# P transposes and softmax sums moved behind the eighth K tile of a decode-attention batch

## The chip, the cores and the metric

The kernel runs on one core of a Trainium2 chip. The metric is device time in microseconds (us) of that core, the median over several executions. One execution is recorded by the hardware profiler; its trace gives every instruction's start and duration on TensorE (PE, with weight loads apart as PEld), VectorE (DVE), ScalarE (ACT), GpSimd (POOL), and the DMA issues of SyncE (SP).

## The reference

One decode step (one new token) for a batch of 8: pre-norm attention over the last 2048 positions of a KV cache, then an MLP with a shift over tokens, both with residuals. With one token the shifted branch of the MLP is all zeros, so w1 and w2 drop out.

```
x = A_x                                   # [8, 1, 512]
q = layernorm(x) @ wq                     # 32 heads of 128
k, v = last W = 2048 rows of the caches   # 8 kv heads, 4 q heads share one
p = softmax(q k^T / sqrt(128));  o = p v
h = x + o @ wo
xb = layernorm(h)
x1 = xb + 0                               # shift of a length-1 sequence
out = h + x1 + gelu(layernorm(x1) @ w3) @ w4
```

All inputs are bfloat16. K and V of one batch are 4.2 MB each (8 heads x 2048 x 128 x 2 bytes), 67 MB for all batches; with wq, wo, w3 and w4 the traffic is 79.18 MB.

## The kernel before

**Loads.** SyncE issues all large loads on one queue, in a fixed order (`sp_prog`, line 234 on): wq, the two K halves of batch 0 (each half is 4 kv heads, 2 MB, one of two slots), then per batch the two K halves of the next batch and the two V halves of this one, at last the rest of wo, w3 and w4. There are two K slots and two V slots. The next load of a K slot waits until TensorE has transposed the tiles in it (`sem_Thi`, waited for ahead of line 246: 4 tiles for the first slot, 8 for the second); a load of a V slot waits until TensorE has used it (`sem_PV`). w4 goes into the first K slot and so waits for the fourth tile of the last batch (line 265).

**A batch on TensorE** (`pe_block`, line 561). A K half is cut into 4 tiles of 16 blocks of 128 positions. `pe_T` (line 438) transposes a tile's 16 blocks into one of two PSUM buffers `kT_ps`; ScalarE copies the lower half to SBUF (`act_Elo`, line 460), VectorE the upper (`dve_Ehi`, line 464). `pe_QK` (line 478) multiplies the transposed tile with the queries, 4 heads side by side, and adds into the scores `S_ps`. After the eighth tile VectorE takes the maximum (`dve_max`, line 487 on), ScalarE the exponential in two halves with row sums (`act_exp`, line 503).

The probabilities of a batch are used one batch later: `pe_P` (line 454) transposes P, 8 blocks a half, into `kT_ps`; `dve_pT` (line 525) multiplies with a mask into `pT_sb`; `pe_LB` (line 510) adds the row sums over partitions and `dve_rL` (line 516) inverts them; `pe_PV` (line 535) multiplies with V; `dve_O1` and `pe_OP` (lines 544, 554) scale and reorder the output, and `act_OP` stores it.

**The order around the change.** The program of each engine is written out by hand as a list. TensorE's batch is a loop body; its waits (`need`, line 421) consume semaphores by constants, so that the body is the same in each pass. Before the change TensorE's order in a batch is: tiles 0 to 3; P halves 0 and 1; sums; scores of tiles 0 and 1; then tiles 4 to 7, each followed by the scores of the tile two before; scores 6 and 7; PV and output of the last batch. VectorE copies tiles 0 to 3, does both mask multiplies and the reciprocal, and copies tiles 4 to 7. As `pe_P` writes into `kT_ps`, tiles 4 and 5 wait for the mask multiplies (`sem_pT`).

After the loop come the last batch's P, PV and output (`pe_last`), the projection with wo (line 668), the norms, w3 (line 733), gelu, and w4 (line 761).

Of the kernel before, what the change touches and what calls it, by code (L numbers as in the profile page):

```python
# [28 lines left out]
NT = 4  # L29
# [7 lines left out]
def bass_sequential_preLN__sliding_block_cached__mixer_s_mlp__decode_kernel(  # L37
# [24 lines left out]
    with es:  # L62
# [99 lines left out]
        sem_pT = S("sem_pT")  # L162
# [110 lines left out]
        PE, AC, DV = [], [], []  # L273
# [135 lines left out]
        def dve_qc(e, b):  # L409
            e.tensor_copy(qcur[:, :, 32 - R:32], q_all[:, b, :].rearrange("p (g r) -> p g r", r=R)).then_inc(sem_qc, 1)  # L410
# [4 lines left out]
        def need(e, sem, n):  # L415
            d = n - taken.setdefault(sem, 0)
            if d > 0:
                taken[sem] = n
                log.append((sem, d))
                if e is not None:  # L420
                    e.wait_ge(sem, d).then_inc(sem, -d)  # L421

        def pe_T(e, i, t):
            p = 2 * NT * i + t
            gq = t // NT
            if t % NT == 0:
                need(e, sem_k[gq], 16 * (i + 1))
            if t in (4, 5):
                need(e, sem_pT, 2 * i + t - 3)
            elif t in (2, 3, 6, 7):  # L430
                need(e, sem_Elo, p - 1)
                need(e, sem_Ehi, p - 1)
            if e is None:
                return
            k0 = t % NT * CT * DH
            src = slots[:, gq, k0:k0 + CT * DH]
            for c in range(CT):
                ins = e.matmul(kT_ps[t % 2][:, c * 128:(c + 1) * 128], src[:, c * 128:(c + 1) * 128],  # L438
                               perm_b[:, :], is_transpose=True)
                if c == CT // 2 - 1:  # L440
                    ins.then_inc(sem_Tlo, 1)
                if c == CT - 1:
                    ins.then_inc(sem_Thi, 1)

        def pe_P(e, i, half):
            need(e, sem_exp, 2 * i + half + 1)
            n = min(2 * NT * i + 3 + half, 2 * NT * NB)
            need(e, sem_Elo, n)
            need(e, sem_Ehi, n)
            if e is None:  # L450
                return
            for c in range(CT // 2):
                k = half * CT // 2 + c
                ins = e.matmul(kT_ps[half][:, c * 128:(c + 1) * 128], P_sb[:, k * 128:(k + 1) * 128],  # L454
                               perm_p[:, :], is_transpose=True)
            ins.then_inc(sem_PT, 1)

        def act_Elo(e, i):
            e.wait_ge(sem_Tlo, i + 1)
            e.activation(kT_sb[:, i % NKT, 0:W // 2], kT_ps[i % 2][:, 0:W // 2], ACT.Copy).then_inc(sem_Elo, 1)  # L460

        def dve_Ehi(e, i):
            e.wait_ge(sem_Thi, i + 1)
            e.tensor_copy(kT_sb[:, i % NKT, W // 2:W], kT_ps[i % 2][:, W // 2:W]).then_inc(sem_Ehi, 1)  # L464

        def pe_QK(e, i):
            b, t = divmod(i, 2 * NT)
            gq, qi = divmod(t, NT)
            need(e, sem_Elo, i + 1)
            need(e, sem_Ehi, i + 1)  # L470
            if t == 0:
                need(e, sem_qc, b + 1)
            if e is None:
                return
            kv = kT_sb[:, i % NKT, :].rearrange("d (c g p) -> d g c p", p=PP, g=GL)
            o = 32 - R - R * t
            for gl in range(GL):
                ins = e.matmul(S_ps[32 * gl:32 * (gl + 1), 0, :], qcur[:, GL * gq + gl, o:o + 32],  # L478
                               kv[:, gl, :, :], start=(t == 0), stop=(t == 2 * NT - 1),
                               tile_position=(0, 32 * gl), skip_group_check=True)  # L480
            ins.then_inc(sem_QK, 1)
# [18 lines left out]
        def act_exp(e, b, half):  # L500
            e.wait_ge(sem_max, b + 1)
            n = 512 // 2
            e.activation(P_sb[:, half * W // 2:(half + 1) * W // 2].rearrange("r (k g) -> r k g", g=GL),  # L503
                         bass.AP(tensor=S_ps[:, :, :].tensor, offset=half * n, ap=[[1024, 128], [1, n], [0, GL]]), ACT.Exp,
                         bias=mtile[:, 0, 0:1], scale=1.0, accum_out=lsum[:, half:half + 1]).then_inc(sem_exp, 1)

        def pe_LB(e):
            if e is not None:
                for half in range(2):
                    ins = e.matmul(LB, lspread[:, :, :].rearrange("p q h -> p (q h)"), lsum[:, half:half + 1],  # L510
                                   start=(half == 0), stop=(half == 1))
                ins.then_inc(sem_LB, 1)

        def dve_rL(e, b):
            e.wait_ge(sem_LB, b + 2)
            e.reciprocal(rL[:, :], LB).then_inc(dve_self, 1)
            cnt["dve_self"] += 1

        def dve_pT(e, b, half):
            e.wait_ge(sem_PT, 2 * b + half + 3)  # L520
            if b < 0 and half == 0:
                e.wait_ge(sem_pool, POOL_PT)
            m = mask16[:, :, :]
            h0 = half * CT // 2
            e.tensor_tensor(bass.AP(tensor=pT_sb[:, :, :, :].tensor, offset=h0 * NT * 48,  # L525
                                    ap=[[CT * NT * 48, 128], [48, CT // 2 * NT], [32, 2], [1, 16]]),
                            kT_ps[half][:, 0:W // 2].rearrange("p (c a x) -> p c a x", a=2, x=16),
                            bass.AP(tensor=m.tensor, offset=m.offset, ap=[m.ap[0], [0, CT // 2 * NT], [0, 2], [1, 16]]),
                            ALU.mult).then_inc(sem_pT, 1)

        def pe_PV(e, slot, gq, cs=range(CT)):
            for c in cs:
                for q in range(NT):
                    k = q * CT + c
                    ins = e.matmul(pv_ps[32 * q:32 * (q + 1), :], pT_sb[:, c, q, 16 * gq:16 * gq + 32],  # L535
                                   slots[:, slot, k * DH:(k + 1) * DH], start=(gq == 0 and c == 0),
                                   stop=(gq == 1 and c == CT - 1), tile_position=(0, 32 * q), skip_group_check=True)
            if c == CT - 1:
                ins.then_inc(sem_PV[gq], 1)
# [9 lines left out]
        def pe_OP(e, b):  # L549
            need(e, sem_O1, b + 1)  # L550
            if e is None:
                return
            for q in range(4):
                ins = e.matmul(op_ps(b), selw[:, q, :], o_sum[:, NJ * q:NJ * (q + 1)], start=(q == 0), stop=(q == 3))  # L554
            ins.then_inc(sem_OP, 1)
# [4 lines left out]

        def pe_block(e, i, later=None):
            p = 2 * NT * i
            for t in range(NT):
                pe_T(e, i, t)
            pe_P(e, i, 0)
            pe_P(e, i, 1)
            pe_LB(e)
            pe_QK(e, p)
            pe_QK(e, p + 1)
            for t in range(NT, 2 * NT):  # L570
                pe_T(e, i, t)
                pe_QK(e, p + t - 2)
            pe_QK(e, p + 6)
            pe_QK(e, p + 7)
            if i == 0:
                return
            with nullcontext() if e is None else e.If_ne(later, 0):
                log.append("later")
                for gq in range(2):
                    need(e, sem_v[gq], 16 * i)  # L580
                    if e is not None:
                        pe_PV(e, 2 + gq, gq)
                pe_OP(e, i - 1)
# [18 lines left out]
        for i in range(NB):  # L602
            p = 2 * NT * i
            for t in range(2 * NT):
                AC.append(lambda e, n=p + t: act_Elo(e, n))
                DV.append(lambda e, n=p + t: dve_Ehi(e, n))
                if t == 3:
                    DV.append(lambda e, i=i: dve_pT(e, i - 1, 0))
                    DV.append(lambda e, i=i: dve_pT(e, i - 1, 1))
                    if i:  # L610
                        DV.append(lambda e, i=i: dve_rL(e, i - 1))
            AC.append(lambda e, i=i: act_exp(e, i, 0))
            AC.append(lambda e, i=i: act_exp(e, i, 1))
            DV.append(lambda e, i=i: dve_max(e, i))
            if i + 1 < NB:
                DV.append(lambda e, i=i: dve_qc(e, i + 1))
            if i:
                DV.append(lambda e, i=i: dve_O1(e, i - 1))
                AC.append(lambda e, i=i: act_OP(e, i - 1))
# [211 lines left out]
```

## Time and profile before

| | |
|---|---|
| median of 4 runs | 193.66 us (193.16 to 194.82) |
| the profiled execution's own time | 193.32 us |
| its span, first to last instruction | 191.5 us |
| TensorE busy | 141.9 us (74%) |
| VectorE, ScalarE busy | 85.8 us (45%), 93.3 us (49%) |
| GpSimd busy | 6.4 us (3%) |
| mean granted TensorE clock | 0.916 |

A row of the page's groups names the line, the engine, the operation, what it writes and reads, how often, and the busy time; behind the bar stand the idle time of the engine just before and what ended it. In a timeline the columns are start, duration, engine, line, operation and the number of instructions merged into the row, with the wait before it in brackets. SPq is SyncE's queue of DMA issues, PEq TensorE's sequencer. A slice is a fortieth of the span, its digit the busy share in tenths.

| group | instructions | busy us | mean ns |
|---|---|---|---|
| K tile transposes, line 438 | 1024 | 72.7 | 233 |
| scores, line 478 | 256 | 22.6 | 387 |
| PV, line 535 | 1024 | 16.2 | 219 |
| P transposes, line 454 | 144 | 10.9 | 218 |
| sums, line 510 | 36 | 5.0 | 243 |
| lower copies on ScalarE, line 460 | 64 | 64.8 | 1024 |
| upper copies on VectorE, line 464 | 64 | 44.2 | 691 |
| mask multiplies on VectorE, line 525 | 18 | 12.4 | 687 |

Matmuls overlap in the array, so that the mean of one is longer than the distance between two.

### The profile page before, as it was taken

What the parts mean: (1) busy time and instruction counts of PE and PEld (TensorE: products, weight loads), DVE (VectorE), ACT (ScalarE), POOL (GpSimd) and SP (SyncE); (2) the same over time, 40 slices, a digit from 0 to 9 for tenths busy, and PEclk for the clock granted to TensorE, in tenths of its full rate; (3) what the DMA queues carried; (4) which work ended last, traced back from release to release, by engine and by line L of the source; (5) the groups of instructions that cost most, each with busy time, mean ns of one, the idle gap of its engine ahead of it and who ended that gap; (6) DMA issues with size and microseconds to landing.
All of it is one profiled execution on the core that took longest, in us unless ns stands there. A gap on an engine that the chain in (4) does not pass through costs nothing. (4 is left out here: it accounts for less than half of the span.)

```text
span 191.5 us, 6348 instructions
## 1 busy us (share of the span) xinstructions
PE 141.9 (74%) x2848; PEld 114.8 (60%) x2848; DVE 85.8 (45%) x183; ACT 93.3 (49%) x119; POOL 6.4 (3%) x17
## 2 busy tenths in 40 slices
PE   2037893499859995997499949994997499987664
PEld 0014771487658765774497749674875397676652
DVE  7924745064615461744055514551746045551041
ACT  3032664465466446664284457455854464552041
POOL 8400000000000000000000000000000000000000
PEclk9999999589997999999879996999999979999755
DMA  6999999999999999999999999999999999999991
GB/s 221 438 428 431 424 417 431 435 431 435 431 436 424 421 431 433 431 438 431 435 431 424 424 435 431 438 431 438 428 428 424 431 431 438 435 435 407 409 401 42
DMA packets 6329, 79.31 MB, mean 414 GB/s; under 512 B 672, under 2 KB 688, under 8 KB 1712
## 3 DMA queue, kind: packets, MB, share of 16 engines
q1 hardware_dynamic: 6304, 79.18, 97.2%
q8 instruction: 6, 0.10, 0.2%
q10 hardware_dynamic: 16, 0.01, 0.0%
q14 instruction: 3, 0.02, 0.0%
HBM read 79.18 MB, written 0.01 MB: 413 GB/s over the span
## 5 line engine op out<-in xcount | busy, mean ns | idle before, releaser
L460 ACT ACTIVATE kT_sb<-kT_ps 128x1024 bf16<-128x1024 bf16 x64 | 64.8, 1024 | 50.0 <-PE kT_ps L438 49.7
L438 PE MATMUL kT_ps<-perm_b,slots 128*128 128x128 bf16 x1024 | 72.7, 233 | 17.2 <-PEq L421 17.0
L438 PEld LDWEIGHTS kT_ps<-perm_b,slots 128*128 128x128 bf16 x1024 | 65.2, 105 | 27.7 <-issue 27.4
L464 DVE COPY kT_sb<-kT_ps 128x1024 bf16<-128x1024 bf16 x64 | 44.2, 691 | 68.2 <-PE kT_ps L438 68.2
L503 ACT ACTIVATE P_sb<-S_ps,mtile 128x1024 bf16<-128x1024 f32 x16 | 17.7, 1110 | 19.3 <-DVE mtile L498 19.3
L478 PE MATMUL S_ps<-kT_sb,qcur 128*32 128x512 bf16 x256 | 22.6, 387 | 2.9 <-PEq L421 2.9
L535 PE MATMUL misc<-slots,pT_sb 128*32 128x128 bf16 x1024 | 16.2, 219 | 1.8 <-PEq L421 1.8
L535 PEld LDWEIGHTS misc<-slots,pT_sb 128*32 128x32 bf16 x1024 | 14.7, 97 | 3.3 <-issue 3.2
L525 DVE TENSOR_TENSOR pT_sb<-kT_ps,mask 128x1024 bf16<-128x1024 bf16 x18 | 12.4, 687 | 3.6 <-PE kT_ps L454 3.5
L454 PE MATMUL kT_ps<-perm_p,P_sb 128*128 128x128 bf16 x144 | 10.9, 218 | 3.1 <-PEq L421 3.1
L478 PEld LDWEIGHTS S_ps<-kT_sb,qcur 128*32 128x32 bf16 x256 | 5.5, 93 | 10.1 <-issue 6.6
L454 PEld LDWEIGHTS kT_ps<-perm_p,P_sb 128*128 128x128 bf16 x144 | 8.4, 97 | 5.1 <-issue 4.6
L554 PE MATMUL b<-o_sum,selw 128*128 128x32 f32 x56 | 7.3, 275 | 4.3 <-PEq L421 4.3
L554 PEld LDWEIGHTS b<-o_sum,selw 128*128 128x128 f32 x56 | 6.8, 191 | 5.3 <-issue 5.3
L487 DVE TENSOR_REDUCE mtile<-S_ps 128x1 f32<-128x512 f32 x8 | 5.5, 692 | 5.0 <-PE S_ps L478 5.0
L286 DVE TENSOR_SCALAR ident_f<-iota_f 128x128 f32<-128x128 f32 x1 | 5.7, 5684 | 1.3 <-POOL iota_f L207 1.3
L287 DVE TENSOR_SCALAR ident_b<-iota_f 128x128 bf16<-128x128 f32 x1 | 5.6, 5609 | 0.0
L344 PE MATMUL b<-ident_b,xln_b 8*128 8x8 bf16 x4 | 0.3, 175 | 7.1 <-DVE xln_b L320 7.1
L544 DVE TENSOR_SCALAR o_sum<-misc,rL 128x128 f32<-128x128 f32 x8 | 2.8, 351 | 5.6 <-PE misc L535 5.6
L668 PE MATMUL S_ps<-opl,slots 128*128 128x8 bf16 x128 | 3.6, 167 | 2.0 <-issue 1.8
L510 PE MATMUL S_ps<-lsum,lspread 128*128 128x1 f32 x36 | 5.0, 243 | 0.0
L344 PEld LDWEIGHTS b<-ident_b,xln_b 8*128 8x128 bf16 x4 | 0.2, 115 | 8.0 <-DVE xln_b L320 8.0
(91 smaller groups left out, 64.9 us busy)
## 6 DMA issues: line engine op xcount, KB each, us to landing
slots<-in_A_k_cache_dram SPq DMA_DIRECT2D x16, 2048.0 KB, 13.9
slots<-in_A_v_cache_dram SPq DMA_DIRECT2D x16, 2048.0 KB, 17.9
slots<-in_A_wq_dram SPq DMA_DIRECT2D x1, 4096.0 KB, 12.2
slots<-in_A_wo_dram SPq DMA_DIRECT2D x2, 1024.0 KB, 21.9
slots<-in_A_wo_dram SPq DMA_DIRECT2D x1, 2048.0 KB, 26.7
slots<-in_B_w_dram SPq DMA_DIRECT2D x2, 896.0 KB, 31.5
slots<-in_B_w_dram SPq DMA_DIRECT2D x1, 1024.0 KB, 28.6
slots<-in_B_w_dram SPq DMA_DIRECT2D x1, 512.0 KB, 28.3
```

Of the source, the lines that this page charges most:

```text
L286: e.tensor_single_scalar(ident_f[:], iota_f[:], 0.0, ALU.is_equal)
L287: ins = e.tensor_single_scalar(ident_b[:], iota_f[:], 0.0, ALU.is_equal)
L438: ins = e.matmul(kT_ps[t % 2][:, c * 128:(c + 1) * 128], src[:, c * 128:(c + 1) * 128], perm_b[:, :], is_transpose=True)
L454: ins = e.matmul(kT_ps[half][:, c * 128:(c + 1) * 128], P_sb[:, k * 128:(k + 1) * 128], perm_p[:, :], is_transpose=True)
L460: e.activation(kT_sb[:, i % NKT, 0:W // 2], kT_ps[i % 2][:, 0:W // 2], ACT.Copy).then_inc(sem_Elo, 1)
L464: e.tensor_copy(kT_sb[:, i % NKT, W // 2:W], kT_ps[i % 2][:, W // 2:W]).then_inc(sem_Ehi, 1)
L478: ins = e.matmul(S_ps[32 * gl:32 * (gl + 1), 0, :], qcur[:, GL * gq + gl, o:o + 32], kv[:, gl, :, :], start=(t == 0), stop=(t == 2 * NT - ...
L487: ins = e.tensor_reduce(mtile[:, 1, 0:1], S_ps[:, 0, :], AX.X, ALU.max)
L503: e.activation(P_sb[:, half * W // 2:(half + 1) * W // 2].rearrange("r (k g) -> r k g", g=GL), bass.AP(tensor=S_ps[:, :, :].tensor, offset ...
L525: e.tensor_tensor(bass.AP(tensor=pT_sb[:, :, :, :].tensor, offset=h0 * NT * 48, ap=[[CT * NT * 48, 128], [48, CT // 2 * NT], [32, 2], [1, ...
L535: ins = e.matmul(pv_ps[32 * q:32 * (q + 1), :], pT_sb[:, c, q, 16 * gq:16 * gq + 32], slots[:, slot, k * DH:(k + 1) * DH], start=(gq == 0 ...
L554: ins = e.matmul(op_ps(b), selw[:, q, :], o_sum[:, NJ * q:NJ * (q + 1)], start=(q == 0), stop=(q == 3))
```

## The change

In TensorE's batch the two P halves and the sums leave their place between the fourth and fifth tile. The tiles run from 0 to 7 without a break, from the third on each is followed by the scores of the tile two before; then P half 0, the sums, the scores of tile 6, P half 1, the scores of tile 7. Tiles 4 and 5 no longer wait for the mask multiplies but, as the others, for the copies of the tile two before; P waits for the copies of tiles 6 and 7 in place of 2 and 3. Ahead of PV stands a wait for both mask multiplies. On VectorE the multiplies and the reciprocal stand behind the copy of tile 7, ahead of the maximum.

```
         def pe_T(e, i, t):
...
-            if t in (4, 5):
-                need(e, sem_pT, 2 * i + t - 3)
-            elif t in (2, 3, 6, 7):
+            if t > 1:
                 need(e, sem_Elo, p - 1)
                 need(e, sem_Ehi, p - 1)
...
         def pe_P(e, i, half):
             need(e, sem_exp, 2 * i + half + 1)
-            n = min(2 * NT * i + 3 + half, 2 * NT * NB)
+            n = min(2 * NT * i + 7 + half, 2 * NT * NB)
...
         def pe_block(e, i, later=None):
             p = 2 * NT * i
-            for t in range(NT):
-                pe_T(e, i, t)
-            pe_P(e, i, 0)
-            pe_P(e, i, 1)
-            pe_LB(e)
-            pe_QK(e, p)
-            pe_QK(e, p + 1)
-            for t in range(NT, 2 * NT):
+            pe_T(e, i, 0)
+            pe_T(e, i, 1)
+            for t in range(2, 2 * NT):
                 pe_T(e, i, t)
                 pe_QK(e, p + t - 2)
+            pe_P(e, i, 0)
+            pe_LB(e)
             pe_QK(e, p + 6)
+            pe_P(e, i, 1)
             pe_QK(e, p + 7)
+            need(e, sem_pT, 2 * i + 2)
...
             for t in range(2 * NT):
                 AC.append(lambda e, n=p + t: act_Elo(e, n))
                 DV.append(lambda e, n=p + t: dve_Ehi(e, n))
-                if t == 3:
-                    DV.append(lambda e, i=i: dve_pT(e, i - 1, 0))
-                    DV.append(lambda e, i=i: dve_pT(e, i - 1, 1))
-                    if i:
-                        DV.append(lambda e, i=i: dve_rL(e, i - 1))
+            DV.append(lambda e, i=i: dve_pT(e, i - 1, 0))
+            DV.append(lambda e, i=i: dve_pT(e, i - 1, 1))
+            if i:
+                DV.append(lambda e, i=i: dve_rL(e, i - 1))
```

## The prediction

> **What bounds the kernel now.** I read the page's slices and queues first, then the chain that ended last, then the DMA issues with their landing times, and last the timeline of one batch and of the tail. The slices and the queue of the page:
>
> ```profile
> DMA  6999999999999999999999999999999999999991
> GB/s 221 438 428 431 424 417 431 435 431 435 431 436 424 421 431 433 431 438 431 435 431 424 424 435 431 438 431 438 428 428 424 431 431 438 435 435 407 409 401 42
> q1 hardware_dynamic: 6304, 79.18, 97.2%
> ```
>
> The reader is to see that the 16 DMA engines are full in every slice but the first and the last, at 417 to 438 GB/s until the weights (407, 409, 401). One queue carries the 79.18 MB; at the 430 GB/s that the table of stretches has from 20 to 180 us (last column; the one before it is the engines' busy share) they take 184.1 us of a span of 191.5.
>
> ```profile
> 20.00:180.00 160.00, 128.26 (x2595) 106.05 (x2596) 71.04 (x144) 85.29 (x105) 0.00 (x0) 0.94 1.01 430
> ```
>
> TensorE is busy 74%, and it waits for K at the head of every batch. The end of the chain of waits:
>
> ```profile
> 152.98 5.21 PE kT_ps L438 x64
> 158.19 0.02 issue
> 158.21 1.49 SPq L265
> 159.69 0.04 issue
> 159.73 28.32 DMA slots<-in_B_w_dram
> ```
>
> The chain says that the first four K tiles of the last batch release the w4 loads (line 265), which land 28 us later and end the run. Those 28 us are a queue, not a latency: 512 KB at 430 GB/s are 1.2 us. How long a transfer stands in the queue is in the issues (KB each, median us from issue to landing; the second line is the K load issued at 107.46 alone):
>
> ```profile
> slots<-in_A_k_cache_dram SPq DMA_DIRECT2D x16, 2048.0 KB, 13.9
> slots<-in_A_k_cache_dram SPq DMA_DIRECT2D x1, 2048.0 KB, 11.4
> slots<-in_A_v_cache_dram SPq DMA_DIRECT2D x16, 2048.0 KB, 17.9
> ```
>
> 2048 KB are 2.097 MB, 4.9 us at 430 GB/s. So when the first K load of a batch is issued, 13.9 - 4.9 = 9.0 us of older work is ahead of it; the second has 6.5 us; a V load 9.1 (14.0 for the one issued at 109.74) to 13.0. These are the margins: a slot may come free later by that much before the DMA engines run dry.
>
> **The change part by part.** Nothing is added to or taken from the arithmetic or the traffic: 16 P transposes, 4 passes for the sums, two mask multiplies and one reciprocal per batch all stay. TensorE's waits go from 26 to 25 a batch. ScalarE's order and SyncE's are untouched, GpSimd has nothing in the loop.
>
> *The middle, removed.* In the batch from 94.70 the stage between the fourth and the fifth tile looks so:
>
> ```profile
> 99.86 0.61 PE L454 MATMUL kT_ps<-perm_p,P_sb 128*128 128x128 bf16 x8
> ...
> 100.90 0.61 PE L454 MATMUL kT_ps<-perm_p,P_sb 128*128 128x128 bf16 x8 [0.43 <-PEq L421]
> 101.34 0.56 PE L510 MATMUL S_ps<-lsum,lspread 128*128 128x1 f32 x4
> 101.83 0.62 PE L478 MATMUL S_ps<-kT_sb,qcur 128*32 128x512 bf16 x8
> 102.38 1.07 PE L438 MATMUL kT_ps<-perm_b,slots 128*128 128x128 bf16 x16
> ```
>
> From 99.86 to 102.38 are 2.52 us: two P halves (0.44 each, by the starts 100.90 and 101.34), sums 0.49, two score groups 0.54, and about 0.6 us of waiting. Of the work, only the wait is saved; the rest moves.
>
> *The tiles, run on end.* From 102.38 the tiles follow each other with a score group between them every 1.33 us (102.38, 103.70, 105.03, 106.36). I put T2 to T7 at that pitch. In a batch at full clock (start 133.53) the first two tiles take 1.95 us as in the first batch (32 transposes at 17.96), so T2 starts at 2.0 after the batch's start, T3 at 3.3, T4 at 4.7, T7 at 8.65. Before, T4 began at 6.35 there (139.88) and T7 at 10.34. T4 can't start before the second K load, 4.9 us behind the first: it waits some 0.2 us at most.
>
> *The end, added.* T7 1.0, score group 0.33, P half 0.44, sums 0.49, score 0.3, P half 0.44, score 0.3, and the new wait for the second mask multiply. That multiply takes 0.69 us and starts some 0.2 after its transposes; 0.3 lie under the last scores, so the wait is about 0.6 to 0.7. The trace of before doesn't show this wait. From below it is zero (both multiplies done before the scores are); from above I take 1.7 us, the multiply with a second one queued ahead of it (2 x 0.69) and 0.3 of signalling. I take 0.7, since each of its parts has a row. Sum 4.0: PV begins at 8.65 + 4.0 = 12.65, against 146.13 - 133.53 = 12.60 before. Queued behind the wait on TensorE are the PV matmuls, the output step and the next batch's tiles; behind the multiplies on VectorE stand the reciprocal (0.16) and the maximum, which before started 0.17 after PV did and now starts 0.2 after. So the batch is as long as before to 0.1 us, bounds -0.6 (the whole middle wait gained, nothing lost) and +1.1 (the wait at 1.7 instead of 0.7). In a batch that starts at half clock a score group more falls into the slow stretch; I put up to +0.4 there.
>
> The heads of two batches in the table of stretches (TensorE's granted clock is the third number from the end):
>
> ```profile
> 133.50:137.50 4.00, 3.95 (x65) 3.69 (x66) 2.08 (x3) 3.29 (x4) 0.00 (x0) 1.00 0.98 418
> 152.95:156.95 4.00, 3.97 (x48) 4.00 (x48) 1.36 (x2) 2.24 (x3) 0.00 (x0) 0.65 0.98 418
> ```
>
> The first came after a pause of TensorE of 1.8 us, the second after 2.1; four tiles took 3.9 us in the one and 5.2 in the other. [...]
>
> *What that does to SyncE's queue.* The first K slot is released after T3: T3 ends at 4.35 instead of 3.9, 0.45 later (0.7 at half clock), of a margin of 9.0. The second after T7: some 1.7 us earlier. The V slots: with PV, 0.1 to 0.4 later, of 9.1 or more. Nothing comes near to emptying the queue; an earlier issue only lengthens it. So every load lands when it landed before. That is the cover for all edits; were it gone, each batch would pay its 0.1 to 0.4 us, 7 times, 0.7 to 2.8.
>
> [...]
>
> *The tail.* After the last landing only w4 work is left. TensorE's weight loads there:
>
> ```profile
> 186.93 0.77 PEld L761 LDWEIGHTS b<-slots,gT 128*8 128x8 bf16 x32 [0.64 <-ACT gT L744]
> 188.09 0.31 PEld L761 LDWEIGHTS b<-slots,gT 128*8 128x8 bf16 x16 [0.39 <-DMA slots<-in_B_w_dram]
> 188.73 0.10 PEld L761 LDWEIGHTS b<-slots,gT 128*8 128x8 bf16 x8 [0.32 <-DMA slots<-in_B_w_dram]
> ```
>
> The first of three pieces waited for ScalarE's gT, that is for the computed chain; the second and third for DMA, 0.39 and 0.32 us. So the computed chain of the last batch (scores, softmax, PV, projection, norms, w3, gelu) has 0.7 us to spare, and above that every microsecond of delay shows. It can't gain: the third piece lands when it lands. The last batch's delay is 0.1 to 0.4 (its clock came back after 2.8 us), under 0.7. PV's second half can't start before the last V load anyway, 3 x 4.9 = 14.7 us behind the first K load, which pulls early batches back to the same point. Sum: 0.0 us on a span of 191.5 and the profiled run's own time of 193.32 (1.82 beside the span); the median of the four runs, 193.66, lies 0.34 above that, and I forecast 193.6. The bounds on the tail: -0 and 1.1 - 0.7 = +0.4 at full clock, 1.5 - 0.7 = +0.8 with the 0.4 of half clock.
>
> **The rivals.**
>
> *The w4 loads follow their release.* The chain of waits taken at its word: T3 of the last batch ends 0.45 to 0.7 later, and so does everything behind it: 194.1 to 194.4. Against it: when they are issued (158.21) the w3 loads, issued at 152, still have until about 183.5 (31.5 us) to land. Within 1%.
>
> *The last batch runs at half clock, and the tail shows it.* Which batches start at half clock is not set by their code, as the two heads above show. If the clock stayed low through all eight tiles of the last batch, the four-tile difference of 5.2 - 3.9 = 1.3 us comes twice, 2.6, with up to 0.5 on P and scores (half of their 1.0 of streaming) and the new wait's upper 1.0: 2.6 to 4.1, less 0.7 to spare: +1.9 to +3.4, 195.5 to 197.0. It decides from a delay of 0.7 + 1.9 = 2.6 us in the last batch. For it: the change moves TensorE's pauses. Against: the granted clock is 0.94 from 20 to 180 us, and the two heads lose their low stretch within 4 us or so.
>
> *TensorE's order held the transfers up, and the change frees them.* Then the second K load, issued 1.7 us earlier in 7 batches, would give up to 11.9 us, 181.7. Against it stands the DMA row: there is no idle slice to fill; the gap between 97.2% and full is 5.4 us, nearly all in the first 1.7 and the last 2.8 us, which the change doesn't touch. I see no more than 1 us there.
>
> **How the numbers follow.** Nothing shows: 0.68, 193.6. Delay of the tail of under 1% by one of the first two ways or by a wait that I sized too low: 0.14, around 194.5. Half clock or another wait of several us in the tail: 0.13, around 196. The transfers are freed: 0.05, under 191.7. A measurement of this kernel tells about 1% from no change (its four runs go from 193.16 to 194.82), so faster 0.05, same 0.82, slower 0.13. The range takes the runs' own scatter below (193.0, with 0.2 for another chip), and reaches above to the start of the slow rival: 192.8 to 195.4.
>
> **What would show it.** In the changed profile the DMA row stays at 9 in every slice but the ends and moves 430 GB/s from 20 to 180 us; tiles of line 438 come eight in a row at 1.33 us; PV waits some 0.7 us for VectorE; the K loads' median to landing goes from 13.9 to a little over it for the second and under it for the first; the last w4 piece lands at 188.7. I'd be wrong if a slice of DMA falls to 8 in the loop, if the weight loads of the first w4 piece start after 187.7, or if a batch's head no longer waits for K.

## The result, and the profile after

| | before | after |
|---|---|---|
| median | 193.61 us (63 executions, 192.95 to 196.11) | 193.24 us (42 executions, 192.98 to 194.33) |
| above 193.7 us | 30 of 63, mean 194.51 | 5 of 42, mean 193.99 |
| mean of the others | 193.21 us | 193.20 us |
| the profiled execution | 193.32 us, span 191.5 | 193.09 us, span 191.3 |

The ratio of the times is 0.9974, with a 95% interval of 0.9961 to 0.9987. That is within 1%, as forecast, but it is not nothing: the means are 193.83 and 193.29 us, 0.54 apart, and the medians 0.37. The table says where it is. The usual execution takes as long as before (193.21 and 193.20), and fewer executions are late. I call an execution late when it takes over 193.7 us; I drew that line after seeing the times.

The slices and the queue of the page of after, the columns as in the prediction:

```profile
DMA  6999999999999999999999999999999999999991
GB/s 221 438 428 425 425 416 437 432 438 435 425 427 421 432 435 437 435 435 418 435 418 438 435 438 432 432 425 428 425 435 438 435 435 421 432 421 428 407 409 54
...
q1 hardware_dynamic: 6304, 79.18, 97.4%
```

The same stretch of the loop in the table of stretches:

```profile
20.00:180.00 160.00, 132.16 (x2633) 108.23 (x2632) 71.69 (x146) 86.92 (x106) 0.00 (x0) 0.94 1.01 430
```

The row of nines is the same, the rate is 430 GB/s as before. TensorE shows 132.16 us busy where it was 128.26, and 38 more matmuls (2633 against 2595). Both pages count 2848 matmuls in all: the stretch cuts the two programs at different places. Part of the busy time is in how it is added up: two score groups in one row took 0.62 us before, each alone takes 0.40 now. The limit has not moved.

Now the last batch on TensorE, from its timeline:

```profile
153.06 3.02 PE L436 MATMUL kT_ps<-perm_b,slots 128*128 128x128 bf16 x48 [1.38 <-PEq L421]
...
156.34 1.07 PE L436 MATMUL kT_ps<-perm_b,slots 128*128 128x128 bf16 x16
...
158.26 1.05 PE L436 MATMUL kT_ps<-perm_b,slots 128*128 128x128 bf16 x16 [0.53 <-PEq L421]
159.25 0.40 PE L476 MATMUL S_ps<-kT_sb,qcur 128*32 128x512 bf16 x4
159.58 1.07 PE L436 MATMUL kT_ps<-perm_b,slots 128*128 128x128 bf16 x16
...
163.57 0.62 PE L452 MATMUL kT_ps<-perm_p,P_sb 128*128 128x128 bf16 x8
...
166.62 2.11 PE L533 MATMUL misc<-slots,pT_sb 128*32 128x128 bf16 x128 [0.83 <-PEq L421]
```

The tiles run on (158.26, 159.58, then 160.91 and 162.24: 1.33 us apart). The stage of 2.52 us in the middle is gone. The fifth tile waits 0.53 us for the second K load and for the semaphores behind it, P stands behind the eighth tile, and PV (line 533) waits 0.83 us from the last scores on, first for the mask multiply. The page has this wait as 5.8 us over the loop.

SyncE's issues of the K loads in the same batch, first before, then after (start, time from the first to the end of the second):

```profile
119.47 7.98 SPq L246 DMA_DIRECT2D slots<-in_A_k_cache_dram  x2
```

```profile
119.63 5.85 SPq L246 DMA_DIRECT2D slots<-in_A_k_cache_dram  x2
```

The second K load is now issued 5.85 - 7.98 = 2.13 us nearer to the first. The issues with their time to landing, on the page of after:

```profile
slots<-in_A_k_cache_dram SPq DMA_DIRECT2D x16, 2048.0 KB, 13.5
slots<-in_A_v_cache_dram SPq DMA_DIRECT2D x16, 2048.0 KB, 17.1
```

They were 13.9 and 17.9. The tail's weight loads on TensorE, after:

```profile
186.72 0.77 PEld L757 LDWEIGHTS b<-slots,gT 128*8 128x8 bf16 x32 [0.92 <-ACT gT L740]
187.88 0.31 PEld L757 LDWEIGHTS b<-slots,gT 128*8 128x8 bf16 x16 [0.40 <-DMA slots<-in_B_w_dram]
188.51 0.10 PEld L757 LDWEIGHTS b<-slots,gT 128*8 128x8 bf16 x8 [0.32 <-DMA slots<-in_B_w_dram]
```

They are the three pieces of before, 0.21 us earlier, with the same two waits for DMA (0.40 and 0.32). The chain that ended last has the same end too:

```profile
158.26 1.07 PE kT_ps L436 x16
159.33 0.43 SPq L265
159.76 0.04 issue
159.81 28.03 DMA slots<-in_B_w_dram
```

So the question for the experiments was not the limit but the late executions: what makes one, and why does the change make fewer?

### The profile page after: what moved, and what is told of

Same layout as the page of the kernel before. It is cut to its first block, busy times and chain, and to the rows that moved or that the text cites. A ratio compares the mean times of both kernels' runs of the same rounds, so it can differ in the third digit from the quotient of the medians.

```text
span 191.3 us, 6340 instructions
## 1 busy us (share of the span) xinstructions
PE 145.5 (76%) x2848; PEld 116.7 (61%) x2848; DVE 85.7 (45%) x183; ACT 94.1 (49%) x119; POOL 6.4 (3%) x17
## 5 line engine op out<-in xcount | busy, mean ns | idle before, releaser
L436 PE MATMUL kT_ps<-perm_b,slots 128*128 128x128 bf16 x1024 | 74.2, 234 | 15.3 <-PEq L421 14.7
L476 PE MATMUL S_ps<-kT_sb,qcur 128*32 128x512 bf16 x256 | 25.7, 392 | 0.0
L476 PEld LDWEIGHTS S_ps<-kT_sb,qcur 128*32 128x32 bf16 x256 | 6.6, 93 | 6.0 <-issue 0.2
L367 PE MATMUL S_ps<-slots,xlnT 128*8 128x512 bf16 x32 | 3.6, 628 | 1.8 <-DMA slots<-in_A_wq_dram 1.8
## 6 DMA issues: line engine op xcount, KB each, us to landing
slots<-in_A_k_cache_dram SPq DMA_DIRECT2D x16, 2048.0 KB, 13.5
```

## The experiments

Two explanations stood against each other. The computed chain is the work from the last batch's scores to w4; the transfers are SyncE's loads. **Late chain:** in a late execution the computed chain of the last batch (softmax, PV, projection, norms, w3, gelu) reaches w4 too late. **Late transfers:** SyncE issues a K load of the second batch so late that the queue runs dry near 30 us, and each later transfer lands late. Names that begin with b are the kernel before with an edit, with a the kernel after. Each time is held against unedited executions of the kernel before on the same chip.

**1. The kernel before again** (b_again), to see its own scatter.

> The kernel of before, unchanged. Theory A (slack of the tail): the transfers end at the same time in both kernels, and the kernel of before has more executions in which the computed chain of the last batch comes later than the last w4 load can hide; so about half of its executions should lie at 193.0 to 193.5 and the rest at 193.7 to 195, and a profiled one of the second kind should show the first w4 matmuls starting after 187.7 us with the loads landing as before. Theory B (the transfers run earlier in the changed kernel): every execution is longer by 0.3 to 0.5 and the K loads of the later batches land later. Theory C (chance): ratio 1.000, no two groups.

Measured: 193.26 us, ratio 0.9993 [0.9959, 1.0027]; 3 of 10 above 193.7, and 9 of 22 of its comparison. The late executions belong to the kernel before, on this chip too.

**2. Warm heads with bfloat16 matmuls** (b_warm):

```
+            pe_dummy(e, 20)      # pe_block: 20 matmuls of 128 columns at the head of a batch
```

> The kernel of before with 20 unused 128-column transposing-size matmuls on TensorE at the head of each batch, where it waits for K (1.1 us at full clock of a wait of 1.8). Theory A1 (the late executions are those in which the last batch starts at half clock): the four-tile head takes 3.9 us in every batch, the granted clock of the loop goes from 0.94 to near 1.0, and the second group is gone: ratio 0.997, as the changed kernel. Theory A2 (the late executions come from the tail behind the loop, not from the clock): clock higher, ratio 1.00. Theory B: 1.00.

Measured: 195.28 us, 1.0103 [1.0066, 1.0141], 1.0% longer; all 4 above 193.7. Its timeline of TensorE:

```profile
183.54 0.22 PE L675 MATMUL S_ps<-opl,slots 128*128 128x8 bf16 x2 [2.40 <-issue]
...
188.80 1.67 PE L768 MATMUL b<-slots,gT 128*8 128x128 bf16 x56
```

In the projection TensorE stood 2.40 us and waited for nothing that the profile shows, in addition to the pause of 1.2 to 2.0 us that most of these kernels have there. The w4 matmuls then began at 188.80 and ran through in 1.67 us: all weights were there, the chain was late. The experiment changed more than it meant to, and does not tell the two explanations apart.

**3. A shorter last PV** (b_short leaves out 60 of the 64 matmuls of the last batch's second V half):

```
-            pe_PV(e, 5, 1)
+            pe_PV(e, 5, 1, range(CT - 1, CT))
```

> The kernel of before with 60 of the 64 matmuls of the last batch's second V half left out, so the computed chain behind the loop is 0.9 us shorter and nothing in the loop changes. The output lacks that part of the sum. Theory A: the tail's slack goes from 0.7 to 1.6 us; most of the second group goes, ratio 0.996 to 0.998, lowest time unchanged at 193.0. Theory B: ratio 1.000. Theory C: 1.000.

Measured: 193.3 us, 1.0002 [0.9982, 1.0022]; 2 of 10 above 193.7. The time that PV gave up went into new waits in the projection:

```profile
177.02 2.10 PE L668 MATMUL S_ps<-opl,slots 128*128 128x8 bf16 x64 [0.75 <-DMA slots<-in_A_wo_dram]
180.15 1.01 PE L668 MATMUL S_ps<-opl,slots 128*128 128x8 bf16 x32 [1.03 <-DMA slots<-in_A_wo_dram]
```

Two waits, 0.75 and 1.03 us, for the wo loads. An earlier chain does not lower the usual time: the transfers hold the floor, the least time that the loads allow (lowest execution 193.03, 193.01 in its comparison). Whether fewer executions are late (2 of 10 against 9 of 22) these numbers do not tell.

**4. A later last PV** (a_late):

```
+            pe_dummy(e, 18)      # pe_last: ahead of the last pe_PV
             pe_PV(e, 5, 1)
```

> The changed kernel with 18 unused matmuls ahead of the last batch's second V half, 1.0 us more in the computed chain behind the loop. Theory A: the gain goes back or more, since the slack it had won is used up: ratio to the kernel of before 1.000 to 1.004, with executions above 193.7 again. Theory B: the gain stays, 0.997. Theory C: 1.000 as before.

Measured: 194.53 us, 1.0054 [1.0022, 1.0085]; all 7 above 193.7. The tail of its timeline:

```profile
184.00 0.48 PE L689 MATMUL S_ps<-hcat,mean_w 128*128 128x64 f32 x2 [2.39 <-issue]
...
188.31 1.67 PE L764 MATMUL b<-slots,gT 128*8 128x128 bf16 x56
```

A second pause again, 2.39 us, and w4 began 188.31 - 186.75 = 1.56 us later than in after. Most of that is the pause: the projection ended only 0.54 us later (181.61 against 181.07), since the first pause took up part of the delay. The profiled execution took 194.18, that is 1.09 more. So 1.56 - 1.09 = 0.47 us were to spare: with all weights there the w4 matmuls take 1.67 us, with the waits 2.15, and the difference of 0.48 is the slack. A late chain costs what exceeds it.

**5 and 6. Two more profiles of the kernel before** (b_look1, b_look2), one execution each, to find a late one.

> The kernel of before, unchanged, for one profile of an execution above 193.7 us, of which it has about four in ten. Theory A1 (clock): in such a profile the last batch stays at half clock for a second 3.4 us stretch, its chain is 1 us later or more, and the first w4 matmuls start after 187.7. Theory A3 (code): TensorE's pauses without a releaser behind the loop (1.5 to 1.8 us at line 668) are longer, or there is a second one, with the last batch as in the profile of before. Theory B: the loads land later.

> As the look before it: a second chance of an execution above 193.7 us, with the same marks of the three theories.

Measured: 194.31 and 193.12, one of each kind. Of 19 comparison executions 8 were above 193.7. In the late one, the weight loads of w4:

```profile
187.87 0.77 PEld L761 LDWEIGHTS b<-slots,gT 128*8 128x8 bf16 x32 [1.40 <-issue]
189.03 0.31 PEld L761 LDWEIGHTS b<-slots,gT 128*8 128x8 bf16 x16 [0.40 <-DMA slots<-in_B_w_dram]
189.64 0.11 PEld L761 LDWEIGHTS b<-slots,gT 128*8 128x8 bf16 x8 [0.30 <-DMA slots<-in_B_w_dram]
```

All three pieces are 1.1 us later than in the other execution (186.73, 187.89, 188.53). The same row on TensorE's own timeline has 1.15 us of waiting for the w4 transfer. The chain was not late: the last PV began at 171.73, in after at 171.72. This is an execution with late transfers. The K loads of its second batch, then those of b_look2:

```profile
23.71 7.98 SPq L246 DMA_DIRECT2D slots<-in_A_k_cache_dram  x2
```

```profile
22.45 8.00 SPq L246 DMA_DIRECT2D slots<-in_A_k_cache_dram  x2
```

In the late execution the second load was issued by 31.69, in the other by 30.45. At 34.3 us the records of b_look1 show nine packets of 16 KB (a packet is a piece of a load, as the trace records it) that took 0.76 to 2.10 us instead of 0.61. I read this as the first engines having reached the end of their queue; no row shows it.

Each load lands in 16 shares: the traces record 16 landings for it, and the kernel waits for all 16 (`e.wait_ge(sem_vl[1], 16)`). In after the shares of the last batch's second K load land from 156.07 to 157.82, and TensorE's wait for it ends at 157.85. The landing records say where b_look1 lost its time. From the second batch's second K load on its shares land on average 0.57 us later than those of b_look2 (40.34 against 39.77), and still so in the second of the three wo loads (176.57 against 176.00): the time lost near 34 us does not come back. But the last share of each load, for which TensorE waits, is hardly later there: 41.12 against 41.14, 177.24 against 177.19. It comes late in the second half of w3. Fifteen shares have landed by 184.41 and the last by 185.32, 0.91 us behind them (184.19 in b_look2), and the w4 loads stay late from there. One packet of the instruction queue, 0.92 us from 181.98 on, lies in that stretch. Whether it held up this share, and whether this execution would have been in time without the loss at 34 us, is not shown.

**7. Code places moved** (a_shift): 18 matmuls of 8 columns at the start of the kernel after, so that the code behind them lies elsewhere.

```
+            for _ in range(18):
+                e.matmul(misc[:, 160:168], ident_b[:, :], perm_b[:, 0:8], start=True, stop=True, ...)
```

> The changed kernel with 18 unused 8-column matmuls on TensorE at the start, where it waits for wq: no delay to anything, but the 36 instructions move every later place in TensorE's code. [...] If the delay in the run with the late chain came from its 18 matmuls alone, the ratio here is 0.997.

Measured: 193.11 us, 0.9988 [0.9968, 1.0008]; 2 of 10 above 193.7. But the edit did not move the pause. The projection in the profile of before, then in a_shift:

```profile
176.17 0.61 PE L668 MATMUL S_ps<-opl,slots 128*128 128x8 bf16 x18 [0.22 <-ACT opl L559]
178.55 3.02 PE L668 MATMUL S_ps<-opl,slots 128*128 128x8 bf16 x110 [1.77 <-issue]
```

```profile
176.53 0.61 PE L667 MATMUL S_ps<-opl,slots 128*128 128x8 bf16 x18 [0.22 <-ACT opl L560]
178.75 3.07 PE L667 MATMUL S_ps<-opl,slots 128*128 128x8 bf16 x110 [1.61 <-issue]
```

TensorE stops behind the 18th matmul of the projection in both, and in every other profile whose edit lies ahead of the loop. Edits in the loop or behind it do move it: b_warm, with 20 more matmuls and their weight loads in the loop body, stops 20 matmuls earlier, a_late 18 earlier. The second pause of each comes exactly 128 matmuls behind the first, which in both is at the end of the projection, where everything behind it waits. At the old place the 128 end among the w3 matmuls, where no pause shows. So the moved pause is most of what made experiments 2 and 4 late, and a_shift does not test it.

**8. Warm heads with two fp32 matmuls** (b_warm2):

```
+                for _ in range(2):       # pe_block, ahead of the first tile
+                    e.matmul(S_ps[:, 1, 64:384], ident_f[:, :], selw[...][:, 0:320], ...)
```

> The kernel of before with two unused 320-column fp32 matmuls at each batch's head in place of the 20 small ones of the earlier run: 1.1 us of TensorE work at full clock, but only 8 instructions, so that the code places behind the loop move by 4 pairs and not by 20. Theory A1 (clock): heads at full clock, the executions above 193.7 go, ratio 0.997. Theory A3 (code): the executions above 193.7 stay, ratio 1.00.

Measured: 193.16 us, 0.9974 [0.9949, 0.9999]; none of 10 above 193.7. Granted clock 0.949 in the profiled execution, heads of 3.93 to 4.38 us. The kernel before reaches the change's ratio if TensorE is kept busy ahead of its heads (the first four tiles of a batch). But in this profile the second K load of the second batch was issued by 25.12 + 7.98 = 33.1, later than in b_look1, and packets near 34 us were stretched there too (eleven, by 3.0 us in all, against nine by 7.6): a late issue is not enough for a late execution.

**9. An earlier clock at the start** (b_early): 19 matmuls on zeros while wq is loading.

```
+            for _ in range(15):          # pe_zinit; four more at the end of pe_pro1
+                e.matmul(misc[:, :], zrow_b[0:1, :], x_sb[0:1, :], start=True, stop=True)
```

> The kernel of before with 19 unused one-row 512-column matmuls on TensorE while it waits for x and wq, so that its clock is up before the first K tile; nothing else is changed. Theory D (the second K load of batch 1 is issued late in the executions in which the clock comes up only at 21.5 us; the DMA engines that lead then stand at 34 us): the clock is released before 17 us in every execution, the load is issued at 29.4 to 30.2, no 16 KB packet at 34 to 35 us takes longer than the others, and the executions above 193.7 us fall from four in ten to one in ten or less: ratio 0.997, as the changed kernel has it. Theory A (the computed chain of the last batch is late): share and ratio as before, 1.000.

Measured: 193.85 us, 1.0009 [0.9985, 1.0033]; 7 of 12 above 193.7. The expectation of late transfers failed: the first four tiles of the first batch took 4.03 us instead of the 5.42 of b_look1, no packet was stretched, and still most executions were late. The profiled one, 193.92, is of the other kind. The head of its last batch in the table of stretches (length, TensorE's busy time, granted clock, DMA share, GB/s):

```profile
153.00:155.00 2.00, 1.83 (x18) 0.50 0.99 426
155.00:157.00 2.00, 2.00 (x22) 0.50 1.05 451
157.00:159.00 2.00, 2.00 (x22) 0.50 0.97 418
159.00:161.00 2.00, 1.54 (x26) 0.96 0.98 418
```

and what became of it on TensorE:

```profile
153.17 6.58 PE L442 MATMUL kT_ps<-perm_b,slots 128*128 128x128 bf16 x64 [2.11 <-PEq L425]
...
168.42 1.97 PE L539 MATMUL misc<-slots,pT_sb 128*32 128x128 bf16 x128
...
177.75 0.61 PE L672 MATMUL S_ps<-opl,slots 128*128 128x8 bf16 x18 [0.22 <-ACT opl L563]
...
188.05 1.67 PE L765 MATMUL b<-slots,gT 128*8 128x128 bf16 x56
```

The clock stayed at 0.50 through all four tiles. They took 6.58 us instead of 3.93, PV began 15.25 us after the head, the projection at 177.75 instead of 175.92 in b_look1, and the w4 matmuls ran without a wait from 188.05. That is a late chain.

**10 and 11. A later start** (b_start with 8, a_start with 18 matmuls of 512 columns ahead of the first batch):

```
+            for _ in range(8):           # pe_qT; 18 in a_start
+                e.matmul(misc[:, :], ident_b[:, :], q_sb[:, 0, :], start=True, stop=True, ...)
```

> The kernel of before with 8 unused 512-column matmuls (1.7 us at full clock) ahead of the first batch, so that the second K load of batch 1 is issued at 31.2 to 33 us instead of 29.5 to 31.4. Theory D: nearly every execution now has the stretched packets, and most lie above 193.7: ratio 1.003 to 1.006. Theory A: 1.000.

> The changed kernel with 18 unused 512-column matmuls (3.8 us at full clock) on TensorE ahead of the first batch, so that the second K load of batch 1 is issued at about 32 us instead of 29.7; batch 1 and all later ones wait for K as before. Theory D: packets at 33 to 35 us are stretched as in the look at 194.31 us, and half of the executions or more lie above 193.7: ratio to the kernel of before 1.000 or over, 1.003 or more over the changed kernel. Theory A: the last batch is untouched, ratio 0.997.

Measured: b_start 194.18 us, 1.0021 [0.9992, 1.005], 8 of 12 above 193.7; a_start 194.74, 1.006 [1.0031, 1.0088], all 9. The K loads of the second batch and the last w4 piece in a_start:

```profile
28.68 5.85 SPq L246 DMA_DIRECT2D slots<-in_A_k_cache_dram  x2
```

```profile
190.16 0.11 PEld L759 LDWEIGHTS b<-slots,gT 128*8 128x8 bf16 x8 [0.33 <-DMA slots<-in_B_w_dram]
```

The first load was issued 4.7 us later than in after (23.97), 28 packets were stretched near 30 and 35 us, and the last piece was loaded 190.16 - 188.51 = 1.65 us later. Here every load stays late: in the second wo load the shares land on average 1.54 us later than in after, and the last of them 1.37 (178.65 against 177.28). The late transfers can be forced, in the kernel after as well.

**12. Warm heads, but not in the first batch** (b_warm3): the edit of experiment 8 under a condition that leaves the first batch out.

```
+                with e.If_ne(later, 0):
+                    ...
```

> The kernel before with two fp32 matmuls of 320 columns at the head of every batch but the first (the first eight tiles run as in the kernel before; b_warm2 had them there too). Four rows of profiles that are at hand: of the kernel before the eight K transposes' first four tiles took 3.93 to 3.96, 5.2 to 5.4 or 6.5 us at the heads of its batches, and where the last batch had 6.58 (b_early's profile, 193.92) PV began 15.25 us after the head instead of 12.6 and the projection at 177.75 instead of 175.9; b_warm2 had heads of 3.93 to 4.38 and no execution of 10 above 193.7, while 8 of 19 of the kernel before on the same chip were. Theory H (the late executions come from heads at half clock in the later batches, the last one above all): heads of 3.9 to 4.4 from the second batch on, no or one execution of 12 above 193.7, ratio 0.995 to 0.999. Theory S (they come from the start: the first batch at half clock lets the second K load of the second batch be issued late, the queue runs dry and all later loads land late, as in b_look1): the start is that of the kernel before, so 3 to 6 of 12 are above 193.7, ratio 0.999 to 1.002. Either way the lowest time stays 192.9 to 193.1.

Measured: 193.38 us, 0.9995 [0.9973, 1.0017]; 4 of 12 above 193.7, with 7 of 17 in the comparison. By the numbers expected this speaks for the start. It is weaker than that, for the profile (192.97) shows a side effect:

```profile
172.66 3.61 PE L535 MATMUL misc<-slots,pT_sb 128*32 128x128 bf16 x128
...
178.33 3.72 PE L674 MATMUL S_ps<-opl,slots 128*128 128x8 bf16 x128 [0.22 <-ACT opl L559]
...
187.10 1.67 PE L767 MATMUL b<-slots,gT 128*8 128x128 bf16 x56
```

All heads from the third batch on ran at full clock (3.93 us), but the last PV then took 3.61 us for 128 matmuls instead of 2.12: the granted clock was 0.50 from 172.6 to 176.3 us. The projection began at 178.33, later than in b_early, and the execution was in time all the same; the usual pause in the projection is missing. The four late executions may be late chains of this sort.

What follows from the twelve: an execution of the kernel before is late by a late chain or by late transfers. Both were seen in unforced profiles (b_early's last batch, whose edit lies at the start, and b_look1) and both were forced (a_late, mostly by its second pause, and a_start). That a late start makes late transfers is shown for a_start; for b_look1 the link from 34 us to w3 is not shown, and b_warm2 had the late issue without the late end. How often each happens was not settled, and so it is not settled either by which of them the change has fewer late executions.

## Why the prediction was right, and where it was not

**The floor: right.** It was said that full DMA engines set the time and that no edit would move a landing. Apart from b_warm, a_late and a_start, the lowest execution of every kernel lies between 192.94 and 193.13, that of b_short with its 60 matmuls fewer too (193.03).

**The middle and the tiles: right.** The pitch of 1.33 us and the end of the middle wait came as worked out. The second K load is released 2.1 us nearer to the first (1.7 us earlier were forecast). The median to landing became 13.5, a little less than I expected.

**The batch's length: mis-sized.** "So the batch is as long as before to 0.1 us" was wrong by 0.9 at full clock. Over the profiled batches from the third on (without b_warm, b_warm2 and b_warm3, which have work ahead of the heads), by the length of the head (four tiles before, three after) and PV's start behind the head:

| clock at the head | before: head, PV at | after: head, PV at |
|---|---|---|
| full | 3.93 to 3.96, 12.57 to 12.61 | 3.02 to 3.05, 13.51 to 13.57 |
| half in part | 5.19 to 5.46, 13.83 to 14.10 | 4.12 to 4.47, 14.08 to 14.44 |
| half throughout | 6.42 to 6.58, 15.06 to 15.25 | 5.28, 15.46 to 15.47 |

PV was forecast at 12.65 and came at 13.56 in the last batch. Of the 0.91, 0.53 arise by the eighth tile's start (9.18 instead of 8.65), nearly all at the fifth tile. The load itself was no later than worked out: its last share landed at 157.82, 4.76 us after the batch's start and 0.1 behind the moment at which TensorE could have used it. But the tile started at 158.26. Behind the wait for K stand two more semaphore waits, for the copies, long satisfied; the three took their turn 0.15 us apart only when K was there. The forecast had no term for that. The other 0.38 lie behind it (4.38 instead of 4.0): 0.13 in the new wait (0.83 instead of 0.7), the rest in P's second half and the last two scores. My upper bound for a batch, +1.1, held. The named cover held as well. In b_look1, at full clock, PV's second half waits 0.94 us for its V load, which lands at 167.53; after, PV starts 0.98 later and runs through without that wait. It ends at 168.75 and 168.73, and the projection starts at 175.92 and 175.91.

**The slack of the tail: mis-sized.** "0.7 us to spare" summed two waits of the weight loads. The matmuls show 2.15 - 1.67 = 0.48, and a_late 0.47.

**The new wait: right** in place and nearly in size (0.83, 0.7 forecast, bounds 0 and 1.7), but in part by luck. The mask multiply ended 0.40 us into it, at 166.19; the other 0.43 are again what TensorE's sequencer takes in turn behind the wait, here a semaphore, a branch and the semaphore of V.

**The tail's "sum: 0.0 us" and "can't gain": the step that failed.** It took one profiled execution for all. It holds for the usual ones (193.21 and 193.20), but the median of before has 30 late executions of 63 in it, and my text read the 0.34 us between profile and median as scatter that stays. The change made them rarer, and the median fell by 0.37 us.

**The rivals.** *Last batch at half clock* is real, but it happens to the kernel before: b_early's head took 6.58 us, 2.65 more than at full clock, and that is what the rival priced for eight slow tiles (2 x 1.3 = 2.6), in four. The text had this as a danger of the change alone. After the change such a batch would be no shorter (15.46 against 15.06 to 15.25), and none of the profiles of after had it as the last batch. *TensorE's order held the transfers up* was given up to 1 us; the earlier release of the second K load may be such a gain at the one place where the queue is short, near 30 us. In after the first batch began slowly (three tiles in 4.24 us, 3.02 at full clock), as in b_look1, and the second K load was issued by 29.98 instead of 31.69, with no stretched packets at 34 us. Against the profile of before, whose first batch ran at full clock, it is 29.98 against 30.08. That this is what makes late executions rarer was argued, not shown. *The w4 loads follow their release*: no. SyncE's first w4 issue starts at 157.44, at 158.21 before and at 157.03 in b_look1; the chain's piece lands at 159.81 + 28.03 = 187.84, at 188.05 and at 188.99. The earliest release has the latest landing.

## What to carry to other kernels

Where the transfers set the time, look at all executions before the mean of them: a change that leaves the floor alone can still change how often an execution misses it. Two numbers then count, the slack of the computed chain at the end (here 0.5 us) and how short the queue gets at the start, and each can be tested by an edit that pushes it over the edge. Read slack from the instructions that need the data, run with and without the wait, not from a sum of waits. When a wait becomes the last to end, count the sequencer's instructions behind it too: here they took about 0.4 us of each of the two new waits. And find out whether an edit moved what it was meant to move, here a pause, before its time is read.

## What the runs showed of the hardware

- **Half clock behind short pauses.** In the four profiles of the kernel before, unedited, from the third batch on, pauses of TensorE of 0.6 to 2.1 us ahead of a head were followed by heads of 3.9, 5.2 to 5.4 or 6.5 us: 1.82 us by 3.93 and by 5.36, 0.61 by 5.43. So the length of the pause does not tell which head is slow, and in no profile was a pause before a slow head longer than 2.2 us from the third batch on. In the profiled execution of before the heads go 5.36, 3.96, 5.34, 5.36, 3.96, 5.19, a pattern of three batches, which are 3 x 19.45 = 58.35 us. The trace's records of the granted clock have it at 0.50 in before from 32.91 to 39.73 us, and then from 56.80, 94.35, 114.83 and 152.37 us on for 3.41 us each; in after from 34.95 to 41.77, and from 75.91, 113.45 and 133.93 on for 3.41 each. In both records the changes up to 180 us lie 1 to 12 times 3.41 us apart. What sets the moment of such a stretch was not shown.
- **TensorE stands still in straight code.** In 12 of the 14 profiles TensorE stood 1.2 to 2.0 us in or just ahead of the projection with nothing to wait for, in two of these a second time for 2.4 us, and in b_warm3 and b_short not at all. With 20 matmuls more in the loop body (b_warm) the place came 20 matmuls earlier, with 18 more behind the loop (a_late) 18 earlier, and the second pause of both 128 matmuls with their weight loads behind the first. The page has an instruction queue (q8: 6 packets, 0.10 MB) beside the full data queue, and in a_late the second pause runs from 181.61 to 184.00 with such a packet from 181.75 to 182.68. What makes these pauses was not shown.
- **In b_look1 most shares came late, and the last one did not.** In the records of before the 16 shares of one load land within 0.5 us at 18 us, and from 24 us to the last V load over 1.6 to 1.9 us. In b_look1, behind the stretched packets at 34 us, the shares land on average 0.57 us later than in b_look2, at 40 us as at 176, but until 177 us the last share no more than 0.1 us later. TensorE waits for the last share, and so these 0.57 us did not show in its waits until then: the head of the last batch starts at 153.07, at 153.01 in b_look2.
